# Whole rows of x in DRAM: four gathers per job, square turns on VectorE, and the stores of x issued by SyncE

## The chip, the core and the metric

The kernel runs on one core of a Trainium2 chip. The metric is the device time of one execution in microseconds; a profiled execution gives the span and the trace. A core has five engines that run their own instruction streams and wait for one another by semaphores: TensorE (PE; its weight loads are PEld), VectorE (DVE), ScalarE (ACT), GpSimd (POOL) and SyncE (SP). Data moves between DRAM and SBUF by DMA, on 16 DMA engines of the core.

## The reference, cut to what matters

Two blocks in a row. The first is a retention layer (4 batches, 8 heads, 768 positions, head width 64), the second a mixture of 8 experts over its 3072 output rows x of width 512, in which each token goes to one expert.

```python
for t in range(S):                                    # retention, per batch and head
    state = gamma[None, :, None, None] * state + np.einsum('bhd,bhe->bhde', k[:, :, t], v[:, :, t])
    y[:, :, t] = scale * np.einsum('bhd,bhde->bhe', q[:, :, t], state)
x = np.ascontiguousarray(y.transpose(0, 2, 1, 3)).reshape(B * S, H * D)

logits = x @ w_gate                                   # experts
expert_idx = np.argmax(logits, axis=1)
gate_w = probs[np.arange(N), expert_idx]              # softmax of logits
for e in range(E):                                    # x_sorted: rows of x sorted by expert
    h = np.maximum(x_sorted[lo:hi] @ w1[e], 0.0)      # 512 x 1024
    y_sorted[lo:hi] = h @ w2[e]                       # 1024 x 512
out = gate_w[:, None] * y_sorted[inv_perm]
```

## The kernel before

Attention runs in 24 steps (6 stretches of 128 positions times 4 batches). Each step leaves x transposed, features on partitions (`xTg`); VectorE turns its 32x32 blocks into `xg`, and after every four steps ScalarE's queue stores 1 MB of it to DRAM (`x_d`), as quarter rows of 128 numbers. `place` finds the expert and the place of each token. Then there is one job per expert: its rows are gathered from `x_d` by GpSimd, turned on VectorE into `xT`, and go through two layers on TensorE. One expert's gather is 16 indirect DMAs, each of 128 quarter rows. The first two experts' first 256 slots (`EARLY`) are gathered when five of the six groups of tokens are placed, and expert 0's early half runs its first layer while the last group is being placed. TensorE, ScalarE, GpSimd and VectorE keep the order of the text (`manual_schedule`); SyncE's order is the scheduler's.

```python
    L = 32
    Q = P // L
    x_d = dram.tile([N * Q, DT * L], F32, tag="x_d", name="x_d")
    # ... (cut)
    xs2 = [first.tile([P, W // L, DT * L], F32, tag=f"xs{i}", name=f"xs{i}") for i in range(2)]

    def gather(xs, idx, blocks, rows=N * Q):
        for b in blocks:
            nc.gpsimd.indirect_dma_start(
                out=xs[:, b, :], out_offset=None, in_=x_d[0:rows, :],
                in_offset=bass.IndirectOffsetOnAxis(ap=idx[:, b : b + 1], axis=0), bounds_check=rows - 1,
                oob_is_err=False)

    def tables(got, name):
        m = got.shape[2]
        hl = rt([P, 2, m], f"hl{name}", BF16)
        nc.vector.tensor_copy(hl, got[:, 0:2, :])
        ip = ps("tr", 3, "ip")[:, 0 : Q * 2 * m].rearrange("p (g i m) -> p g i m", g=Q, i=2)
        for g in range(Q):
            nc.tensor.matmul(ip[:, g, :, :].rearrange("p i m -> p (i m)"), lhsT=wrap[:, g, :],
                             rhs=hl[:, :, :].rearrange("p i m -> p (i m)"), start=True, stop=True)
        # ... (cut: six VectorE steps from ip to src: four row numbers for every slot)

    def turn(xs, xT, b0, b1):
        for dt in range(DT):
            nc.vector.transpose(xT[:, dt, :], xs[:, b0:b1, ts(dt, L)])

    hp_tags = [("sc", 2), ("sc", 2), ("lg", 1), ("tr", 3)]

    def layer1(n, xT, w1t, hT, f):
        hp = ps(*hp_tags[f % len(hp_tags)], "hp")[:, 0:n]
        for dt in range(DT):
            nc.tensor.matmul(hp, lhsT=w1t[:, 0, dt, ts(f, P)], rhs=xT[:, dt, 0:n], start=(dt == 0),
                             stop=(dt == DT - 1))
        nc.scalar.activation(out=hT[:, f, 0:n], in_=hp, func=AF.Relu)

    # ... (cut)
        def retain(n, then, between):
            c, b = steps[n]
            kt, vs, qT, kT = front.pop(n)
            sc = [ps("sc", 2, "sc").rearrange("p (a t) -> p a t", a=HP) for _ in range(2)]
            am = [att.tile([P, HP, P], F32, tag=f"am{j}", name=f"am{j}") for j in range(2)]
            for a in range(HP):
                for j in range(2):
                    r = ts(j, D)
                    nc.tensor.matmul(sc[j][:, a, :], lhsT=kT[r, a, :], rhs=qT[r, a, :], start=True, stop=True)
            for j in range(2):
                nc.vector.tensor_tensor(out=am[j], in0=sc[j], in1=middle(causal[:, :], HP), op=ALU.mult)
            then()
            # ... (cut: new state; y from the old state)
            between()
            for a in range(HP):
                for j in range(2):
                    nc.tensor.matmul(y[ts(j, D), a, :], lhsT=vs[:, 2 * a + j, :], rhs=am[j][:, a, :], start=(c == 0),
                                     stop=True, skip_group_check=True)
            nc.scalar.copy(out=xTg[n // B % 2][:, :, n % B, :], in_=y)

        def to_rows(n):
            g, b = n // B % 2, n % B
            nc.vector.transpose(xg[g][:, b, :, :].rearrange("p r (a l) -> p a r l", l=L),
                                xTg[g][:, :, b, :].rearrange("p a (r l) -> p a r l", l=L))

        def place(c):
            # ... (cut: logits of four steps, into PSUM tile parts)
            nc.scalar.copy(out=lgT, in_=parts)
            nc.scalar.dma_start(x_d[ts(c, B * P * Q), :].rearrange("(p r) d -> p r d", p=P),
                                xg[c % 2][:, :, :, :].rearrange("p b r d -> p (b r) d"))
            yield
            # ... (cut: expert, rank and place of each token, spread over the later steps; found, inv)
            if c == NC - 2:
                early.append(tables(inv[:, :, 0 : TC + HALF], "_e"))
                for e in range(2):
                    gather(xs2[e], early[0][0][:, e * TC * Q :],
                           range(HALF * Q), (c + 1) * B * P * Q)
    # ... (cut)
        actx.enter_context(tc.manual_schedule(engines={PE, ACT, POOL, DVE}))
        # ... (cut)
        for n in range(len(steps)):
            if n + AHEAD < len(steps):
                load(n + AHEAD)
            if n == len(steps) - AHEAD:
                wa = weights(first, 0)
            if n in (2, 3):
                nc.gpsimd.memset(xs2[n % 2], 0.0)
            if n + 2 < len(steps):
                scale(n + 2)
            # ... (cut: retain(n), with transpose(n + 1), to_rows(n - 1) and the next part of place in it)
        to_rows(len(steps) - 1)
        turn(xs2[0], xTa, 0, HALF * Q)
        cols = []
        for f in range(FT):
            layer1(EARLY, xTa, wa[0], hTa, f)
            if f in (0, 1, 2, 4):
                next(rest, None)
            if f == 3:
                arm, ne = count()
        src, dst, gates = tables(inv, "")
        cols = [(src[:, ts(e, TC * Q)], dst[:, ts(e, TC)], gates[:, ts(e, TC)]) for e in range(E)]
        for e in range(2):
            gather(xs2[e], cols[e][0], range(HALF * Q, TC * Q))
        turn(xs2[0], xTa, HALF * Q, TC * Q)
        layer2(EARLY, hTa, wa[1], oa, 0, early[0][2])
        which = regs(0)
        tc.switch_hint(which, arms_of(0), label="job0")
        layer2(EARLY, hTa, wa[1], oa, 1, early[0][2])
        scatter(oa, early[0][1], range(HALF))
    # ... (cut)
    def rows_of(e):
        xT = mp.tile([P, DT, W], F32, tag="xTs", name="xTs")
        if e > 1:
            gather(xs2[e % 2], cols[e][0], range(TC * Q))
        turn(xs2[e % 2], xT, 0, TC * Q)
        return xT
    # ... (cut)
    with tc.manual_schedule(engines={PE, ACT, POOL}):
        xT, xTn = xTa, rows_of(1)
        for e in range(E):
            last = e + 1 == E
            nxt = None if last else regs(e + 1)
            hT = mp.tile([P, FT, W], F32, tag="hT", name="hT", bufs=1)
            for a in tc.Switch(which, arms_of(e), hint=f"job{e}"):
                job(e, min(STEP * (LEAST + a), W), xT, hT, nxt)
                if last and a == arms_of(e) - 1:
                    further_jobs()
            if not last:
                scatter(o2[e % 2], cols[e][1], range(TC - HALF if e == 0 else TC))
                xT, which = xTn, nxt
            if e + 2 < E:
                xTn = rows_of(e + 2)
                sets.append(weights(first if e % 2 == 0 else keep2, e + 2))
```

## Time and profile before

The median of three runs is 566.6 us (565.68 to 570.61). The profiled execution has a span of 565.0 us.

| what | value |
|---|---|
| TensorE matmuls, busy | 501.0 us, 3008 records |
| GpSimd, busy | 215.1 us |
| VectorE, busy | 124.2 us |
| ScalarE, busy | 104.3 us |
| mean granted TensorE clock | 0.954 |
| gathers of the jobs (L174, src) | 112, 111.9 us of GpSimd |
| gathers of the early halves (L174, src_e) | 16, 16.2 us of GpSimd |
| stores of x (x_d<-xg, from ScalarE's queue) | 6 of 1024 KB, 5.2 us to landing |
| loads of k, v and q (from SyncE) | 24 of 256 KB, 24 of 256 KB, 12 of 512 KB |
| weights (from SyncE) | 16 of 2048 KB |
| DMA packets | 83224, 72.46 MB, of these 54712 under 512 B |

How to read the lines that follow. The page's slices cut the span into 40 equal parts of 14.1 us; a digit is the busy share in tenths, and PEclk is the TensorE clock that was granted. A line of a timeline has the start in us, the time that it covers in us, the engine, the line of the source, the operation, out<-in by the program's names, shapes, the number of instructions that it merges, and in brackets the idle time of the engine just before, with what ended it: an engine's work, a DMA, "issue" (nothing that the profile shows) or "remote" (a semaphore that no recorded instruction set). A line of a group has the count, then the busy time in us and the mean in ns of one, then the idle time before them and what ended most of it. A matmul of 32-bit numbers leaves two records.

### The profile page before, as it was taken

The page shows a single profiled execution, that of the slowest core. Times are in us where ns is not written, and L with a number is a line of the kernel's source. Part 1 is how long each engine was busy: PE and PEld are TensorE (multiplying, and loading weights), DVE is VectorE, ACT ScalarE, POOL GpSimd, SP SyncE. Part 2 cuts the span into 40 slices and gives each one's busy share as a digit, 9 for nine tenths or more (in the row PEclk, how much of TensorE's full clock was granted, in tenths as well). Part 3 has the DMA queues.
Part 4 walks back from the last instruction along what each step waited for, and adds up shares of the span by engine and source line. Part 5 has one row for each costly group of instructions (what it writes and reads, how often), then busy time and mean ns, then how long its engine had stood idle before and what let it go on. Part 6 is the DMA issues. An engine that isn't in the chain of part 4 may idle for free. (4 is left out here: it accounts for less than half of the span.)

```text
span 565.0 us, 7708 instructions
## 1 busy us (share of the span) xinstructions
PE 501.0 (89%) x3008; PEld 300.6 (53%) x3008; DVE 124.2 (22%) x356; ACT 104.3 (18%) x204; POOL 215.1 (38%) x232
## 2 busy tenths in 40 slices
PE   5998999996189959989969999999998899799992
PEld 4776888875156545544534454455454345345540
DVE  2468667675137110010010001000100100100000
ACT  2433242331011111120111012011011101011200
POOL 4744334414601734700760174057157007602010
PEclk9999999999579979989998999999999799999997
DMA  9999999911117118104610650192371047101010
GB/s 207 224 238 233 240 263 274 271 75 27 48 75 281 54 50 317 43 2 151 235 33 2 196 199 13 46 323 56 111 254 38 2 152 240 32 5 55 1 41 21
DMA packets 83224, 72.46 MB, mean 128 GB/s; under 512 B 54712, under 2 KB 67004, under 8 KB 82369
## 3 DMA queue, kind: packets, MB, share of 16 engines
q1 hardware_dynamic: 75472, 52.45, 34.4%
q0 software_dynamic: 6656, 12.61, 7.0%
q10 hardware_dynamic: 1008, 6.34, 3.0%
q8 instruction: 42, 0.69, 0.5%
q14 instruction: 46, 0.37, 0.2%
HBM read 60.88 MB, written 14.68 MB: 134 GB/s over the span
## 5 line engine op out<-in xcount | busy, mean ns | idle before, releaser
L247 PE MATMUL ye<-w2t,hT 128*128 128x512 f32 (+3 forms) x640 | 175.9, 481 | 16.4 <-issue 13.1
L235 PE MATMUL hp<-xTs,w1t 128*128 128x416 f32 (+3 forms) x448 | 154.4, 505 | 0.1
L247 PEld LDWEIGHTS ye<-w2t,hT 128*128 128x128 f32 (+3 forms) x640 | 79.6, 164 | 110.0 <-issue 104.6
L174 POOL DMA_INDIRECT xs<-x_d,src x112 | 111.9, 999 | 60.8 <-issue 33.8
L235 PEld LDWEIGHTS hp<-xTs,w1t 128*128 128x128 f32 x448 | 85.0, 190 | 69.6 <-issue 54.3
L257 POOL DMA_INDIRECT out_dram<-o,dst x30 | 29.8, 995 | 197.9 <-ACT o L253 169.7
L228 DVE STREAM_TRANSPOSE xTs<-xs 128x512 f32<-128x512 f32 x28 | 17.4, 680 | 284.8 <-DMA xs<-x_d,src 233.3
L237 ACT ACTIVATE hT<-hp 128x416 f32<-128x416 f32 (+4 forms) x64 | 29.1, 481 | 165.8 <-issue 75.9
L335 POOL TENSOR_TENSOR vs<-v,dec 128x512 f32<-128x512 f32 x23 | 25.3, 1102 | 55.0 <-DMA v<-in_v_dram 17.0
L235 PE MATMUL hp<-xTa,w1t 128*128 128x256 f32 (+1 forms) x128 | 27.5, 378 | 19.2 <-issue 11.2
L253 ACT ACTIVATE o<-ye,gate 128x512 f32<-128x512 f32 (+1 forms) x22 | 15.1, 687 | 125.8 <-PE ye L247 120.4
L361 DVE TENSOR_TENSOR am<-sc,causal 128x512 f32<-128x512 f32 x48 | 30.8, 681 | 32.0 <-PE sc L359 25.8
L388 PE MATMUL y<-am,vs 128*64 128x128 f32 x384 | 30.3, 291 | 5.8 <-issue 4.7
L235 PEld LDWEIGHTS hp<-xTa,w1t 128*128 128x128 f32 x128 | 22.7, 225 | 23.9 <-issue 14.0
L359 PE MATMUL sc<-qT,kT 64*128 64x128 f32 x384 | 28.8, 291 | 1.4 <-ACT qT L347 0.7
L388 PEld LDWEIGHTS y<-am,vs 128*64 128x64 f32 x384 | 23.0, 143 | 10.7 <-issue 6.1
L359 PEld LDWEIGHTS sc<-qT,kT 64*128 64x128 f32 x384 | 24.1, 193 | 4.9 <-issue 2.7
L390 ACT COPY xTg<-y 128x512 f32<-128x512 f32 x24 | 14.1, 586 | 66.0 <-PE y L388 44.6
L332 POOL TENSOR_TENSOR qs<-q,dec 128x512 f32<-128x512 f32 x22 | 22.5, 1043 | 7.7 <-DMA q<-in_q_dram 7.4
L174 POOL DMA_INDIRECT xs<-x_d,src_e x16 | 16.2, 1014 | 18.7 <-DVE at_e L210 14.2
L383 PE MATMUL y<-qT,state 64*64 64x128 f32 x320 | 21.8, 275 | 0.0
L321 PE MATMUL tr<-ident,k 128*128 128x128 f32 x96 | 16.2, 292 | 4.5 <-DMA k<-in_k_dram 4.5
(147 smaller groups left out, 273.9 us busy)
## 6 DMA issues: line engine op xcount, KB each, us to landing
w1t<-in_moe_w_dram SPq DMA_DIRECT2D x8, 2048.0 KB, 9.2
w2t<-in_moe_w_dram SPq DMA_DIRECT2D x8, 2048.0 KB, 14.3
k<-in_k_dram SPq DMA_DIRECT2D x24, 256.0 KB, 6.0
q<-in_q_dram SPq DMA_DIRECT2D x12, 512.0 KB, 5.7
v<-in_v_dram SPq DMA_DIRECT2D x24, 256.0 KB, 6.0
x_d<-xg ACTq DMA_DIRECT2D x6, 1024.0 KB, 5.2
xs<-x_d,src POOLq DMA_INDIRECT x112
out_dram<-o,dst POOLq DMA_INDIRECT x30
```

Of the source, the lines that this page charges most:

```text
L174: nc.gpsimd.indirect_dma_start(out=xs[:, b, :], out_offset=None, in_=x_d[0:rows, :], in_offset=bass.IndirectOffsetOnAxis(ap=idx[:, b : b + ...
L228: nc.vector.transpose(xT[:, dt, :], xs[:, b0:b1, ts(dt, L)])
L235: nc.tensor.matmul(hp, lhsT=w1t[:, 0, dt, ts(f, P)], rhs=xT[:, dt, 0:n], start=(dt == 0), stop=(dt == DT - 1))
L237: nc.scalar.activation(out=hT[:, f, 0:n], in_=hp, func=AF.Relu)
L247: nc.tensor.matmul(y[j * m : j * m + m, 0:c], lhsT=hT[:, f, t * P : t * P + m], rhs=w2t[:, 0, f, ts(j, c)], start=(f == 0), stop=(f == FT ...
L257: done = nc.gpsimd.indirect_dma_start(out=out[:, :], out_offset=bass.IndirectOffsetOnAxis(ap=idx[:, t : t + 1], axis=0), in_=o[:, t, :], i ...
L332: mul.tensor_tensor(out=qs[:, e, :, :], in0=got["q"][:, :, ts(e, D)], in1=inner(dec[:, ts(c + e, H)], D), op=ALU.mult)
L335: mul.tensor_tensor(out=vs, in0=got["v"], in1=inner(dec[:, ts(NC + c, H)], D), op=ALU.mult)
L359: nc.tensor.matmul(sc[j][:, a, :], lhsT=kT[r, a, :], rhs=qT[r, a, :], start=True, stop=True)
L361: nc.vector.tensor_tensor(out=am[j], in0=sc[j], in1=middle(causal[:, :], HP), op=ALU.mult)
L383: nc.tensor.matmul(y[r, a, :], lhsT=old[r, a, :], rhs=qT[r, a, :], start=(a == 0), stop=False, skip_group_check=True)
L388: nc.tensor.matmul(y[ts(j, D), a, :], lhsT=vs[:, 2 * a + j, :], rhs=am[j][:, a, :], start=(c == 0), stop=True, skip_group_check=True)
```

## The change

`x_d` now holds whole rows: 3072 rows of 512 numbers (2 KB) in place of 12288 quarter rows. A gather of 128 whole rows is one indirect DMA, so a job needs four of them instead of 16, and only one row number per slot instead of four: the four small matmuls with `wrap` and several VectorE steps of `tables` are not needed. What arrives has tokens on partitions, 512 features along the row, with the features in the order in which the stores left them. The 128-partition turns of before do not serve for this layout. A job's `xT` is made by 16 square turns on VectorE, one for each pair of a quadrant of 32 partitions to read and one to write. For expert 0's early half it is made in another way: two copies `xe` on VectorE that put the features in order, eight 128x128 turns on TensorE, and two copies out of PSUM. Expert 1's rows go to a buffer of their own (`xT1`), turned in two halves, so that its turn is no longer part of `rows_of`.

To get whole rows into DRAM, a store of four steps becomes four DMAs, one per quadrant of `xg`, each from 32 partitions in pieces of 128 numbers. They are issued by SyncE and no longer by ScalarE, at a fixed place among the loads, since SyncE's order is now that of the text too. The first expert's weights are loaded two steps later in the text, behind all loads of k, q and v. The diff, cut:

```diff
@@ -89,8 +89,7 @@
     Q = P // L
 
-
-    x_d = dram.tile([N * Q, DT * L], F32, tag="x_d", name="x_d")
+    x_d = dram.tile([N, Q * DT * L], F32, tag="x_d", name="x_d")
 
 
@@ -133,20 +132,12 @@
     row_i, row_r, row_l, tile_4 = (rt([P, 1], "row_i", I32), rt([P, 1], "row_r", I32), rt([P, 1], "row_l", I32),
                                    rt([P, NT], "tile_4"))
-    quarter = rt([P, 1], "quarter")
... (cut)
-
-    wrap = rt([P, Q, P], "wrap", BF16)
-    nc.gpsimd.memset(wrap, 1.0)
-    nc.gpsimd.affine_select(out=wrap[:, :, :].rearrange("p g (a l) -> p g a l", l=L),
-                            in_=wrap[:, :, :].rearrange("p g (a l) -> p g a l", l=L), compare_op=ALU.is_equal,
-                            fill=0.0, base=0, pattern=[[-L, Q], [0, Q], [-1, L]], channel_multiplier=1)
     ohs = rt([P, NT, E], "ohs", BF16)
     ranks = rt([P, NT], "ranks", I32)
@@ -166,54 +157,37 @@
 
     first = ctx.enter_context(tc.tile_pool(name="first", bufs=1))
-    xs2 = [first.tile([P, W // L, DT * L], F32, tag=f"xs{i}", name=f"xs{i}") for i in range(2)]
-
-    def gather(xs, idx, blocks, rows=N * Q):
-
-        for b in blocks:
+    xs2 = [first.tile([P, TC, Q * DT * L], F32, tag=f"xs{i}", name=f"xs{i}") for i in range(2)]
+
+    def gather(xs, idx, tiles, rows=N):
+        for t in tiles:
             nc.gpsimd.indirect_dma_start(
-                out=xs[:, b, :], out_offset=None, in_=x_d[0:rows, :],
-                in_offset=bass.IndirectOffsetOnAxis(ap=idx[:, b : b + 1], axis=0), bounds_check=rows - 1,
+                out=xs[:, t, :], out_offset=None, in_=x_d[0:rows, :],
+                in_offset=bass.IndirectOffsetOnAxis(ap=idx[:, t : t + 1], axis=0), bounds_check=rows - 1,
                 oob_is_err=False)
 
 
         m = got.shape[2]
-        hl = rt([P, 2, m], f"hl{name}", BF16)
-        nc.vector.tensor_copy(hl, got[:, 0:2, :])
-        ip = ps("tr", 3, "ip")[:, 0 : Q * 2 * m].rearrange("p (g i m) -> p g i m", g=Q, i=2)
-        for g in range(Q):
-            nc.tensor.matmul(ip[:, g, :, :].rearrange("p i m -> p (i m)"), lhsT=wrap[:, g, :],
-                             rhs=hl[:, :, :].rearrange("p i m -> p (i m)"), start=True, stop=True)
... (cut: removed, the six VectorE steps from ip to src)
-        return (src,) + targets(got, name)
-
-    def targets(got, name):
+        tok, far = rt([P, m], f"tok{name}"), rt([P, m], f"far{name}")
+        src = rt([P, m], f"src{name}", U32)
+        nc.vector.tensor_scalar(out=far, in0=got[:, 0, :], scalar1=1.0, scalar2=float(FAR), op0=ALU.is_lt, op1=ALU.mult)
+        nc.vector.tensor_tensor(out=far, in0=got[:, 1, :], in1=far, op=ALU.add)
+        nc.vector.scalar_tensor_tensor(out=tok, in0=got[:, 0, :], scalar=float(L), in1=far, op0=ALU.mult, op1=ALU.add)
+        nc.vector.tensor_scalar(out=src, in0=tok, scalar1=-float(L), scalar2=None, op0=ALU.add)
+        return (src,) + targets(got, far, name)
+
+    def targets(got, far, name):
... (cut: far is now made in tables)
@@ -222,10 +196,14 @@
         return dst, gate
 
-    def turn(xs, xT, b0, b1):
-
-        for dt in range(DT):
-            nc.vector.transpose(xT[:, dt, :], xs[:, b0:b1, ts(dt, L)])
+    def turn(xs, xT, tiles):
+
+        n = len(tiles)
+        for r in range(Q):
+            for g in range(Q):
+                nc.vector.transpose(
+                    xT[ts(g, L), :, 0 : n * P].rearrange("p a (t r i) -> p r t a i", r=Q, i=L)[:, r, :, :, :],
+                    xs[ts(r, L), tiles[0] : tiles[0] + n, ts(g, P)].rearrange("p t (a i) -> p t a i", i=L))
 
     hp_tags = [("sc", 2), ("sc", 2), ("lg", 1), ("tr", 3)]
@@ -408,8 +386,9 @@
             lgT = att.tile([P, B * P], F32, tag="lgT", name="lgT", bufs=1)
             nc.scalar.copy(out=lgT, in_=parts)
-            nc.scalar.dma_start(x_d[ts(c, B * P * Q), :].rearrange("(p r) d -> p r d", p=P),
-                                xg[c % 2][:, :, :, :].rearrange("p b r d -> p (b r) d"))
+            for g in range(Q):
+                nc.sync.dma_start(x_d[ts(c, B * P), ts(g, P)].rearrange("(t l) r -> l t r", l=L),
+                                  xg[c % 2][ts(g, L), :, :, :].rearrange("p b q r -> p (b q) r"))
             yield
             lg = ps("lg", 1, "lg")[:, 0 : B * E].rearrange("p (b e) -> p b e", e=E)
@@ -490,8 +469,7 @@
                 early.append(tables(inv[:, :, 0 : TC + HALF], "_e"))
                 for e in range(2):
-                    gather(xs2[e], early[0][0][:, e * TC * Q :],
-                           range(HALF * Q), (c + 1) * B * P * Q)
+                    gather(xs2[e], early[0][0][:, e * TC :], range(HALF), (c + 1) * B * P)
 
                 tot = ps("tr", 3, "tot")[:, 0:2]
@@ -504,19 +482,20 @@
         for n in range(AHEAD):
             load(n)
-        actx.enter_context(tc.manual_schedule(engines={PE, ACT, POOL, DVE}))
+        actx.enter_context(tc.manual_schedule(engines={PE, ACT, POOL, DVE, SP}))
         for n in range(2):
             scale(n)
         nc.sync.dma_start(wg[:, :, 0:E], w_gate.rearrange("(dt p) e -> p dt e", p=P))
         xTa = first.tile([P, DT, EARLY], F32, tag="xTa", name="xTa")
+        xT1 = first.tile([P, DT, W], F32, tag="xT1", name="xT1")
         hTa = keep.tile([P, FT, EARLY], F32, tag="hTa", name="hTa")
         oa = keep.tile([P, EARLY // P, DM], F32, tag="oa", name="oa")
             if n + AHEAD < len(steps):
                 load(n + AHEAD)
-            if n == len(steps) - AHEAD:
+            if n == len(steps) - 3:
                 wa = weights(first, 0)
             if n in (2, 3):
@@ -538,10 +517,19 @@
                 rest = place(n // B)
         to_rows(len(steps) - 1)
-        turn(xs2[0], xTa, 0, HALF * Q)
+
+        xe = keep.tile([P, HALF, DM], F32, tag="xe", name="xe")
+        for t in range(HALF):
+            nc.vector.tensor_copy(xe[:, t, :].rearrange("p (a q l) -> p q a l", q=Q, l=L),
+                                  xs2[0][:, t, :].rearrange("p (q a l) -> p q a l", q=Q, l=L))
 
 
         cols = []
+        for t in range(HALF):
+            tr = ps("tr", 3, "tre").rearrange("p (a t) -> p a t", a=DT)
+            for dt in range(DT):
+                nc.tensor.transpose(tr[:, dt, :], xe[:, t, ts(dt, P)], ident)
+            nc.vector.tensor_copy(xTa[:, :, ts(t, P)], tr)
         for f in range(FT):
             layer1(EARLY, xTa, wa[0], hTa, f)
@@ -549,10 +537,12 @@
                 arm, ne = count()
         src, dst, gates = tables(inv, "")
-        cols = [(src[:, ts(e, TC * Q)], dst[:, ts(e, TC)], gates[:, ts(e, TC)]) for e in range(E)]
+        cols = [(src[:, ts(e, TC)], dst[:, ts(e, TC)], gates[:, ts(e, TC)]) for e in range(E)]
         for e in range(2):
-            gather(xs2[e], cols[e][0], range(HALF * Q, TC * Q))
-        turn(xs2[0], xTa, HALF * Q, TC * Q)
+            gather(xs2[e], cols[e][0], range(HALF, TC))
+        turn(xs2[1], xT1, range(HALF))
+        turn(xs2[0], xTa, range(HALF, TC))
+        turn(xs2[1], xT1[:, :, EARLY:], range(HALF, TC))
 
         cols[0] = (None, dst[:, HALF:TC], gates[:, HALF:TC])
@@ -585,9 +575,8 @@
 
         xT = mp.tile([P, DT, W], F32, tag="xTs", name="xTs")
-        if e > 1:
-            gather(xs2[e % 2], cols[e][0], range(TC * Q))
-        turn(xs2[e % 2], xT, 0, TC * Q)
+        gather(xs2[e % 2], cols[e][0], range(TC))
+        turn(xs2[e % 2], xT, range(TC))
         return xT
 
@@ -660,7 +649,7 @@
 
     with tc.manual_schedule(engines={PE, ACT, POOL}):
-        xT, xTn = xTa, rows_of(1)
+        xT, xTn = xTa, xT1
         for e in range(E):
             last = e + 1 == E
```

## The prediction

> **What bounds the kernel now.** I read the page's busy shares and slices first, then the timeline of all engines where the slices dip, then TensorE's timeline through the jobs, then the groups.
>
> ```profile
> PE 501.0 (89%) x3008; PEld 300.6 (53%) x3008; DVE 124.2 (22%) x356; ACT 104.3 (18%) x204; POOL 215.1 (38%) x232
> ...
> PE   5998999996189959989969999999998899799992
> ...
> PEclk9999999999579979989998999999999799999997
> ```
>
> TensorE is the bound: 501 of 565 us, nine tenths in most slices. So a change gains only in the dips: slices 10 and 11 (141 to 155 us), 14 (198 to 212), and the weak ones in the jobs. The granted clock falls to a half in the same places. The chain of waits holds only the last microsecond and does not help.
>
> ```profile
> 138.43 0.58 ACT L390 COPY xTg<-y 128x512 f32<-128x512 f32 x1 [4.89 <-PE sc L359]
> ...
> 142.73 1.40 DVE L361 TENSOR_TENSOR am<-sc,causal 128x512 f32<-128x512 f32 x2 [6.22 <-remote]
> ...
> 143.57 2.58 PE L388 MATMUL y<-am,vs 128*64 128x128 f32 x16 [4.73 <-issue]
> ...
> 152.42 1.00 POOL L174 DMA_INDIRECT xs<-x_d,src_e  x1 [0.30 <-issue]
> ...
> 155.61 0.58 ACT L390 COPY xTg<-y 128x512 f32<-128x512 f32 x1 [16.59 <-remote]
> ...
> 157.37 2.90 PE L235 MATMUL hp<-xTa,w1t 128*128 128x256 f32 x6 [11.22 <-issue]
> ```
>
> This is the end of attention, in order of time. VectorE waits for the scores sc, whose matmuls stand in the trace at 136.66 to 137.8, and starts at 142.73. ScalarE waits for y, whose matmuls end at 146.15, and starts at 155.61. Both wait 5 to 9.5 us longer than any work that I see, and "remote" says that no recorded instruction released them. What does run there is GpSimd: 16 gathers at a pitch of 1.30 us, 132.6 to 153.4. ScalarE wakes 2.2 us after the last one ended. TensorE idles 4.73 + 11.22 = 16 us. The same picture stands at 197 to 203: TensorE idles 6.03 us for ScalarE, which idles 8.75 us on "remote", while 16 gathers and 2 scatters run from 180.4 to 203.5.
>
> ```profile
> 289.34 1.06 PE L247 MATMUL ye<-w2t,hT 128*32 128x128 f32 x27
> 291.37 0.27 PE L247 MATMUL ye<-w2t,hT 128*32 128x128 f32 x1 [0.97 <-issue]
> ...
> 294.21 0.27 PE L247 MATMUL ye<-w2t,hT 128*32 128x128 f32 x1 [1.73 <-issue]
> ...
> 296.31 24.44 PE L247 MATMUL ye<-w2t,hT 128*32 128x128 f32 x80 [0.98 <-issue]
> ...
> 531.80 22.75 PE L247 MATMUL ye<-w2t,hT 128*32 128x128 f32 x112
> ```
>
> These are second layers of jobs of one size (416 rows, 112 matmul records). The last job has no gathers beside it and takes 22.75 us; job 2 takes 290 to 321, 31.2 us, stammers until 296.31, and then runs some us at half clock. The gathers of job 2 end at 293.86. I take gathers on GpSimd as what holds back TensorE's signals: the stalls end about 2 us after the last gather in every case (243.5 after 241.3, 296.3 after 293.9, 441.6 after 439.4). Why is not in the profile.
>
> ```profile
> L174 POOL DMA_INDIRECT xs<-x_d,src x112 | 111.9, 999 | 60.8 <-issue 33.8
> ...
> L257 POOL DMA_INDIRECT out_dram<-o,dst x30 | 29.8, 995 | 197.9 <-ACT o L253 169.7
> L228 DVE STREAM_TRANSPOSE xTs<-xs 128x512 f32<-128x512 f32 x28 | 17.4, 680 | 284.8 <-DMA xs<-x_d,src 233.3
> ```
>
> A gather moves 128 pieces of 512 B and costs GpSimd 999 ns; a scatter moves 128 rows of 2 KB and costs 995. The cost is by instruction, not by bytes.
>
> [...] mean granted clock 0.58 over 138 to 158, 0.81 over 192 to 210. [...]
>
> **The change, part by part.**
>
> *Gathers.* 16 per job become 4 of whole 2 KB rows. At 1.30 us pitch, 20.8 us of GpSimd become 5.2. Both are hidden as GpSimd time; what counts is how long they lie beside TensorE.
>
> *End of attention.* The index table loses four matmuls and some VectorE steps, so the first gather goes at about 131.5 instead of 132.6, and the last ends at 136.7. The rows land by 138.5 (2 us after, as above). Then, at the trace's durations: sc done 137.8, mask 1.3 to 139.2, y 1.1 to 140.4, xTg 0.6 to 141.1, xg 0.7 to 141.8. New on the path: two copies xe, about 0.5 us each (a guess from 0.70 for 512 elements of turn, and the clear of 2048 at 1.76), eight TensorE turns of 128x128 (1.04 us for eight in attention's row), two evictions at about 0.69 (the mask from PSUM took 0.68). The first hp starts at about 145, against 157.37. I add 1 us for a remaining late signal and 2 us for attention itself (below): 148, a gain of 9.5.
>
> *First layer of the early half.* 157.37 to 177.78 = 20.4 us, of which 4.3 us ran at half clock, worth 2.1. Without the index matmuls (0.8) and with 1 us of cold clock left: 18.3 - 0.8 + 0.3 = about 18. Second layer starts near 166 and ends 14 us later, near 180 (191.75 before).
>
> *Turns.* One 128-partition turn of 256 elements takes 0.40 us alone, 0.33 in a row; a 32-partition turn has as many elements per lane. So a half of 16 square turns is 16 x 0.42 = 6.7 us, and a whole job 16 x 0.70 = 11.2 us, against 1.4 and 2.5. The three halves stand in line after the tables (done near 168): 175, 181.5, 188. The second is what job 0 needs: 181.5 against 180, a new wait of 1.5 us. The job turns are hidden: gathers land about 14 us into a job, 11 us of turns end at 25, and jobs take 40 to 54 us.
>
> *Job 0.* Starts 181.5 (192.33 before). Its stall of 6.03 + 0.78, and about 2.6 us lost to the half clock from 202.6 to 209.4, go, but for 1 us. First layer 7.4, second 7.0: job 1 starts near 197.5, against 216.47. Gain so far 19.
>
> *Jobs 1 to 6.* Second layers against what the same shapes take undisturbed (22.75 for 416 rows; 3 x 6.87 = 20.6 for three tiles; 24.0 for 448): 28.0 - 22.75 = 5.2, 31.2 - 22.75 = 8.5, 25.8 - 24.0 = 1.8, 20.6 - 20.6 = 0, 31.8 - 22.75 = 9.0, 24.0 - 20.6 = 3.4. Sum 27.9. The four gathers now end 11 us into the job, inside the first layer, which has PSUM buffers for four columns ahead (4 x 2.8 = 11.2 us). I count 23 of the 28.
>
> *Stores of x.* 6 of 1 MB, pieces of 8 KB from all partitions, become 24 of 256 KB from 32 partitions, pieces of 512 B. In the trace 8 KB pieces took 351 ns (768 of them: 16.8 us of all 16 DMA engines) and 512 B loads 32 ns; 12288 x 32 / 16 = 24.4 us. So +7.6 us of DMA in a front that is at a DMA share of about 1.0 to 110 us. But the 4 MB of the first expert's weights, 13 us, move behind all loads, and from 51 us on SyncE waits for free buffers, not for engines. What suffers is 33 to 50 us, where GpSimd waits for v and q: +2 us.
>
> Sum: 19 + 23 = 42 off 566.6: **525 us**.
>
> **Rivals.** (1) The late signals are not the gathers' doing, or come with any four of them: then the stalls stay or move into the first layer. For it: scatters (2 KB rows) lie at the start of each job, and the first hT there comes 7.9 us after the job's start against 5.3 in job 7. Against: the stalls' ends follow the last gather. It leaves about 13 us of the gain (earlier rows alone): 550. (2) SyncE or the DMA engines become attention's bound, since stores wait in the line of the loads [...]. For it: DMA share of 1.0 now. Against: stores land only after data that the loads no longer need, and weights leave that stretch. It costs perhaps 10 to 15 us: 538. (3) VectorE becomes the bound between the halves: if a square turn costs 0.7 rather than 0.42, job 0 waits 9 us more and the clock drops: 536. (4) All stalls go: 516.
>
> **Range and chances.** The middle is 525; (4) and a faster tail give 511 as low end, (2) or (3) or half of (1) give 548 as high end. Slower by 2% would need attention to lose 50 us. Faster by over 2% (below 555) 0.91, within 2% 0.06, slower 0.03.
>
> **What would show it.** Right: 32 gathers in the group, of about 1.0 us; no "remote" waits over 3 us on ScalarE; first hp near 148; second layers of 416 rows near 23 us in every job; clock at 1.0 through the jobs; a row of turns of 32 partitions near 0.4 and 0.7 us. Wrong: stalls of TensorE that stay in the second layers though no gather runs; GpSimd's waits for v and q growing before 60 us; TensorE waiting for xTa.

## The result, and the profile after

The changed kernel takes 519.86 us (median of 4; 518.46 to 521.32) against 566.71 us: ratio 0.916, 95% interval 0.912 to 0.9205. The prediction was 525, in 511 to 548. The stalls that it read off the profile are gone. But the experiments will show that the 46.8 us depend on something outside the program: beside some of them the kernel before, unchanged, took 517 us.

Busy time, TensorE's slices and the granted clock, from the page of the changed kernel:

```profile
PE 484.8 (94%) x3008; PEld 293.2 (57%) x3008; DVE 194.4 (38%) x457; ACT 104.5 (20%) x204; POOL 117.9 (23%) x134
...
PE   4998999999789699999999999999999999999991
...
PEclk9999999999999989999999999999999999999996
```

TensorE works as many instructions as before (3008) in 484.8 us instead of 501.0, with a mean granted clock of 0.989 instead of 0.954; the span fell from 565.0 to 516.7. Slices 10, 11 and 13, counted from 0 (129 to 155 and 168 to 181 us), stay weak. In order of time, all engines at the end of attention:

```profile
136.57 1.00 POOL L164 DMA_INDIRECT xs<-x_d,src_e  x1 [0.30 <-issue]
...
138.26 1.29 DVE L339 TENSOR_TENSOR am<-sc,causal 128x512 f32<-128x512 f32 x2 [2.21 <-PE sc L337]
139.10 1.59 PE L366 MATMUL y<-am,vs 128*64 128x128 f32 x16 [0.72 <-DVE am L339]
...
140.73 0.59 ACT L368 COPY xTg<-y 128x512 f32<-128x512 f32 x1 [2.69 <-PE y L366]
...
142.43 1.09 PE L531 MATMUL tre<-ident,xe 128*128 128x128 f32 x8 [1.73 <-DVE xe L523]
```

These answer to the lines of the end of attention before. The last of four gathers ends at 137.57, not 153.42. The mask waits for sc until 138.26, not 142.73. ScalarE copies y at 140.73, not 155.61, and its releaser is a TensorE instruction, not "remote". Next, TensorE's own timeline, with the early half, job 0 and a second layer of 416 rows:

```profile
144.47 1.99 PE L213 MATMUL hp<-xTa,w1t 128*128 128x256 f32 x8 [0.94 <-DVE xTa L532]
...
161.85 13.90 PE L225 MATMUL ye<-w2t,hTa 128*128 128x512 f32 x32
...
179.98 9.01 PE L213 MATMUL hp<-xTa,w1t 128*128 128x128 f32 x64 [4.24 <-DVE xTa L204]
...
263.17 22.75 PE L225 MATMUL ye<-w2t,hT 128*32 128x128 f32 x112
```

The first hp is 12.9 us earlier than before. Job 2's second layer is one unbroken row of 112 matmuls in 22.75 us; before, it stammered for 31.2. A new wait stands ahead of job 0: 4.24 us for a turn of xTa. From the groups:

```profile
L204 DVE STREAM_TRANSPOSE xTs<-xs 32x512 f32<-32x512 f32 x96 | 67.4, 702 | 191.4 <-DMA xs<-x_d,src 190.2
```

The square turns of jobs 2 to 7 take 702 ns each, 11.2 us a job, all of it hidden.

One more view, worked out from the trace's semaphore events: how long after the modelled end of a TensorE instruction its semaphore next rose on record. In the kernel before, some 60 instructions are over 0.5 us late, more than half of them over 3 us, the worst 12.42 us. In the changed kernel there are 9, three over 3 us, the worst 6.03. I call these late signals. The count must not be taken as it stands, because the traces lack events: the kernel before has 340 of TensorE's on record, and a later trace of the same program 358. An event that is missing looks late. ScalarE in job 2 of the kernel before, where the 12.42 us stand:

```profile
274.80 1.33 ACT L237 ACTIVATE hT<-hp 128x416 f32<-128x416 f32 x3 [7.01 <-issue]
278.27 0.52 ACT L237 ACTIVATE hT<-hp 128x416 f32<-128x416 f32 x1 [2.14 <-issue]
...
294.92 0.52 ACT L237 ACTIVATE hT<-hp 128x416 f32<-128x416 f32 x1 [6.51 <-issue]
```

The signal that seems 12.42 us late is that of a column that ended at 275.44, but ScalarE reads this column at 275.61, as the third of the first row. The last line is truly late: its column ended at 289.41, 5.5 us before. So the start of the reader is the surer measure, beside the same read in a trace of the same program in which no signal is late (both kernels have such a trace below). By it, 14 of ScalarE's 72 reads of first-layer columns are over 1 us late in the kernel before, up to 10.3 us; in the changed kernel none is, the worst 0.9. Nor is every stall a wait for a signal: 10.0 us of TensorE's idle time in the kernel before, in 16 pieces, stand ahead of second-layer matmuls that wait for no semaphore, as do the 1.73 us at 294.21 in the prediction's lines.

### The profile page after: what moved, and what is told of

Read it like the earlier page. It is cut to its first block, busy times and chain, and to the rows that moved or that the text cites. A ratio compares the mean times of both kernels' runs of the same rounds, so it can differ in the third digit from the quotient of the medians.

```text
span 516.7 us, 7619 instructions
## 1 busy us (share of the span) xinstructions
PE 484.8 (94%) x3008; PEld 293.2 (57%) x3008; DVE 194.4 (38%) x457; ACT 104.5 (20%) x204; POOL 117.9 (23%) x134
## 5 line engine op out<-in xcount | busy, mean ns | idle before, releaser
L225 PE MATMUL ye<-w2t,hT 128*128 128x512 f32 (+3 forms) x640 | 164.0, 455 | 0.0
L204 DVE STREAM_TRANSPOSE xTs<-xs 32x512 f32<-32x512 f32 x96 | 67.4, 702 | 191.4 <-DMA xs<-x_d,src 190.2
L213 PE MATMUL hp<-xTs,w1t 128*128 128x416 f32 (+3 forms) x384 | 131.9, 504 | 0.0
L225 PEld LDWEIGHTS ye<-w2t,hT 128*128 128x128 f32 (+3 forms) x640 | 74.9, 155 | 86.5 <-issue 85.0
L213 PEld LDWEIGHTS hp<-xTs,w1t 128*128 128x128 f32 x384 | 72.9, 190 | 59.1 <-issue 44.0
L164 POOL DMA_INDIRECT xs<-x_d,src x28 | 28.4, 1014 | 34.9 <-DVE at L186 26.7
L366 PE MATMUL y<-am,vs 128*64 128x128 f32 x384 | 28.6, 281 | 1.6 <-DVE am L339 1.4
L213 PE MATMUL hp<-xTa,w1t 128*128 128x256 f32 (+1 forms) x128 | 24.1, 350 | 5.8 <-DVE xTa L204 4.2
L213 PEld LDWEIGHTS hp<-xTa,w1t 128*128 128x128 f32 x128 | 20.5, 208 | 9.2 <-issue 5.9
L213 PE MATMUL hp<-xT,w1t 128*128 128x416 f32 x64 | 22.5, 512 | 0.0
```

The source lines that it names most:

```text
L164: nc.gpsimd.indirect_dma_start(out=xs[:, t, :], out_offset=None, in_=x_d[0:rows, :], in_offset=bass.IndirectOffsetOnAxis(ap=idx[:, t : t + ...
L204: nc.vector.transpose(xT[ts(g, L), :, 0 : n * P].rearrange("p a (t r i) -> p r t a i", r=Q, i=L)[:, r, :, :, :], xs[ts(r, L), tiles[0] : t ...
L225: nc.tensor.matmul(y[j * m : j * m + m, 0:c], lhsT=hT[:, f, t * P : t * P + m], rhs=w2t[:, 0, f, ts(j, c)], start=(f == 0), stop=(f == FT ...
```

## Experiments

My theory was the prediction's: a run of 16 gathers on GpSimd holds back TensorE's signals. The first four kernels were meant to separate the number of gathers from the rest of the change, and from the mere busyness of GpSimd.

**Sixteen gathers in the new layout.**

```diff
+        quarters = x_d[:, :].rearrange("n (g r) -> (n g) r", g=Q)
         for t in tiles:
-            nc.gpsimd.indirect_dma_start(out=xs[:, t, :], in_=x_d[0:rows, :], ...)
+            for g in range(Q):                                          # index 4 * src + g
+                nc.gpsimd.indirect_dma_start(out=xs[:, t, ts(g, P)], in_=quarters[0 : rows * Q, :], ...)
```

> The changed kernel with each gather of 128 whole rows split into four gathers of 128 quarter rows (512 B), so 16 per job again, same bytes, same layout, same square turns, stores and TensorE turns; three more small VectorE steps per table. Theory (the run of 16 gather instructions on GpSimd, 20.8 us, holds back TensorE's signals): second layers of 416 rows at 28 to 32 us again in jobs 1 to 6 instead of 22.75, some 25 us lost there, and the end of attention waits for the last gather again, some 13 us: about 558 us. Rival (the stalls went for another reason: the whole rows, the square turns, the stores' queue): only the early rows come later, 13 us, second layers stay at 22.75: about 533 us.

**A quarter of the gathers in the kernel before.**

```diff
-        for b in blocks:
+        for b in list(blocks)[::Q]:     # three quarters of the rows of x are left out
```

> The kernel before with only every fourth gather (4 of 16 per job, 128 pieces of 512 B each); the other three quarters of the rows are left out, all else is as it was. Theory: the stalls go without any other part of the change: second layers of 416 rows 22.75 us in every job, no wait over 3 us on ScalarE or VectorE that no instruction released at the end of attention, first hp near 143 to 146: 515 to 525 us. Rival (whole rows, turns or stores are what removed the stalls): the early half starts earlier by up to 13 us, the jobs keep their 28 us: about 550 us.

**Clears on GpSimd in place of gathers**, on the changed kernel:

```diff
         # after the loop of gathers
+        for i in range(5 * len(tiles)):
+            nc.gpsimd.memset(ballast, 0.0)                              # 128 x 800
```

> The changed kernel with five clears of 128x800 on GpSimd after each gather's tile group (20 per job, about 0.75 us each, some 15 us), so that GpSimd is busy as long as with 16 gathers, with no DMA in it. Theory (making gathers, not a busy GpSimd, holds back TensorE's signals): second layers stay at 22.75 us, 520 to 522 us. Rival (any long stretch of work on GpSimd does it): 540 to 560 us.

**Plain transfers by GpSimd in place of gathers**, on the changed kernel:

```diff
         # after the loop of gathers
+        for i in range(3 * len(tiles)):
+            nc.gpsimd.dma_start(plain[:, i, :], x_d[0:P, 0:L])          # 128 pieces of 128 B
```

> The changed kernel with three plain GpSimd transfers (128 pieces of 128 B from fixed rows of x, no index) after each gather, 12 per job beside the four gathers. Theory in its wider form (any transfer that GpSimd issues does it, by its number of pieces): about 1 us each, second layers of 28 us and more again, 540 to 560 us. Narrow form (only gathers by index do it): second layers stay at 22.75 us, 520 to 523 us.

Measured: sixteen gathers 527.52 us, a quarter of the gathers 510.33, clears 521.37, plain transfers 518.29 (12 runs from 514.4 to 520.9). But the kernel before took **516.63 us** beside them, in the same session (kernels run one after the other on one chip), not 566.7, so the ratios to it are 1.021 (1.0168 to 1.0248), 0.990 (0.9861 to 0.9936), 1.010 (1.0072 to 1.0128) and 1.003 (0.9998 to 1.0055). In none of the four traces is a signal over 0.5 us late, and in all the second layers of 416 rows take 22.75 us. By its own numbers my theory fell, since 16 gathers brought no stall; they only bring the rows later (first hp at 149.15, against 144.47 in the changed kernel). Clears and plain transfers could tell nothing, as nothing was late. So I ran the two kernels of the case again, unchanged, and with them an improvement: the turn for job 0 first.

**The kernel before, and the changed kernel, again** (no edit).

> The kernel before, unchanged, once more with a profile, because beside the first experiments it took 516.6 us and not 566.7. New theory: the late signals of TensorE are not in the program alone; on the chip of those experiments even a run of 16 gathers does not bring them. Then the profile shows second layers of 416 rows at 22.75 us in every job, no wait over 3 us without a recorded releaser, a first hp still near 155 because the rows still come after the sixteenth gather, and 515 to 518 us. Rival (my first theory): 16 gathers always bring the stalls, and the time is near 566 us with second layers of 28 to 32 us.

> The changed kernel, unchanged, beside the kernel before on one chip. New theory: where the kernel before has no stalls, the change gives earlier rows and pays square turns: 518 to 521 us against 516.6, that is equal or up to 1 per cent slower. Rival: it stays 8 per cent faster, 520 against 566 us.

**The turn of xTa first.**

```diff
-        turn(xs2[1], xT1, range(HALF))
         turn(xs2[0], xTa, range(HALF, TC))
+        turn(xs2[1], xT1, range(HALF))
```

> The changed kernel with the turn of the second half of job 0 (xTa) put ahead of the turn of the first half of job 1 (xT1), so that job 0 no longer waits for a turn that only job 1 needs. Theory: TensorE's wait of 4.24 us for xTa goes, since its rows land near 168 and 7.2 us of turns end near 175.7, as the second layer does; job 1's two turns end near 190, before job 1 starts: 4 to 6 us less than the changed kernel, 514 to 516 us. Rival (the gathers land too late or job 1 then waits): within 2 us of the changed kernel.

Measured: the kernel before took 516.79 us (24 runs), and its profiled run 517.83; the changed kernel took 519.67, ratio 1.005 (1.0034 to 1.0067): **slower by half a per cent**. The timeline of the kernel before in this run:

```profile
139.83 0.59 ACT L390 COPY xTg<-y 128x512 f32<-128x512 f32 x1 [2.97 <-PE y L388]
...
144.72 3.75 PE L235 MATMUL hp<-xTa,w1t 128*128 128x256 f32 x8 [4.93 <-issue]
...
151.93 1.00 POOL L174 DMA_INDIRECT xs<-x_d,src_e  x1 [0.30 <-issue]
...
263.11 22.75 PE L247 MATMUL ye<-w2t,hT 128*32 128x128 f32 x112
```

It is the same program with the same 16 gathers, of 1.00 us at the same pitch of 1.30. But ScalarE copies y at 139.83 (155.61 in the first trace), TensorE starts the first hp at 144.72, while gathers still run and not near 155 as I expected, and job 2's second layer takes 22.75 us. There is no late signal. TensorE idles 30.2 us, against 64.0 in the first trace, and is busy for 485.9, against 501.0: together the 48.9 us between the spans. So 16 gathers are not enough: something outside the program decides whether they hurt.

The two traces differ in one more thing. The first trace has 2560 packets of 4 bytes for GpSimd's 160 transfers, 16 each, but only 682 events of their landing; here 2556 are on record. In four traces the profile has no time to landing for the gathers: the first ones of both kernels, and below the second one of sixteen gathers and the second one of the mixed loads. All four were taken where the kernel before took 566 us; but where it took as long or longer, the improved kernel (4.5 us) and the one with its stores on ScalarE (4.2 us) have it. What loses the events, and whether the recording itself has a part in the stalls, was not tested.

Turning xTa first gave 516.74 us, 2.9 less than the changed kernel beside it; I had expected 4 to 6. Job 0 in the changed kernel beside it, and with the new order:

```profile
180.32 10.27 PE L213 MATMUL hp<-xTa,w1t 128*128 128x128 f32 x64 [4.24 <-DVE xTa L204]
```

```profile
179.90 7.38 PE L213 MATMUL hp<-xTa,w1t 128*128 128x128 f32 x64 [2.68 <-DVE xTa L204]
```

The wait fell from 4.24 to 2.68 only, because VectorE now waited 5.54 us for the rows of the last gathers, which landed at 172.6 and not near 168. More came from the clock: the same 64 matmuls take 7.38 us, not 10.27. The granted clock at job 0 is at half for 3.413 us in the changed kernel's first profile, for 6.827 here, after the same wait of 4.24 us, and not at all in the new order, which has 3.413 us at the first hp. (At the end of all three spans it is at half again, in the first for 8.1 us.) A half-clock stretch follows a wait of 2.12 us below, and none the wait of 2.68 us here. So a few microseconds come and go for the same wait, and I read differences of that size from the waits, not from totals.

**An improved kernel, and sixteen gathers once more.** VectorE's two clears of o (1.76 us each) stood ahead of the last table step, and so of the gathers that job 0 waits for.

```diff
 # on top of the turn of xTa first
-        nc.vector.memset(t, 0.0)           # the two o tiles
+        nc.gpsimd.memset(t, 0.0)
 # and to_rows(len(steps) - 1) moved from before the two copies xe to after them
```

> The changed kernel with the turn of xTa first, the two clears of o moved from VectorE to GpSimd (they stand ahead of the last table step), and the copies xe ahead of the last turn of xg. Theory: on VectorE 3.5 us of clears go from the path to the last gathers, so these go some 3 to 4 us earlier, their turn ends before TensorE's second layer does, and the 2.7 us that TensorE still waited for xTa go; tre starts some 0.7 us earlier: 512 to 514 us, faster than the changed kernel by 1 per cent or more, and than the kernel before by 0.5 per cent or more where that one takes 517. Rival (GpSimd's clears now hold the gathers, or clears beside the turns slow VectorE): 516 to 518 us.

> The changed kernel with 16 gathers of quarter rows per job once more, on another occasion. What it does is read beside the kernel before. If that one takes 517 us here too, this one takes 524 to 529 us with second layers of 22.75 us. If that one takes 566 us here, the theory that 16 gathers bring late signals there says 550 us or more, with second layers of 28 to 32 us; the rival, that whole rows or square turns removed them, says 524 to 535 us.

Here the kernel before took **566.37 us** (11 runs) again. The improved kernel took 515.47, ratio 0.909 (0.9046 to 0.913), and sixteen gathers in the new layout took **572.05** (one run), as the theory says and the rival does not. The timeline of sixteen gathers, at the end of attention and in job 2:

```profile
153.29 0.99 POOL L166 DMA_INDIRECT xs<-x_d,src_e  x1 [0.30 <-issue]
156.46 0.58 ACT L372 COPY xTg<-y 128x512 f32<-128x512 f32 x1 [17.28 <-remote]
...
289.58 0.99 PE L229 MATMUL ye<-w2t,hT 128*32 128x128 f32 x24
...
295.16 0.40 PE L229 MATMUL ye<-w2t,hT 128*32 128x128 f32 x1 [1.85 <-issue]
296.54 24.40 PE L229 MATMUL ye<-w2t,hT 128*32 128x128 f32 x84 [0.98 <-issue]
```

The marks of the kernel before's first trace are back: "remote" for 17.28 us, ending 2.2 us after the last gather's end, and the stammer in job 2. So in such a session the number of gather instructions brings the late signals (15 reads of first-layer columns are over 1 us late, up to 8.6), whatever the layout, the turns or the stores; the same kernel took 527.52 in the first session, with none.

In the improved kernel, TensorE's timeline:

```profile
143.57 1.99 PE L213 MATMUL hp<-xTa,w1t 128*128 128x256 f32 x8 [1.49 <-DVE xTa L532]
...
176.98 9.01 PE L213 MATMUL hp<-xTa,w1t 128*128 128x128 f32 x64 [2.12 <-DVE xTa L204]
```

The first hp comes 0.9 us earlier than in the changed kernel (144.47), job 0 3.0 us earlier. Not all of the wait went, since VectorE still waits 5.89 us for the rows, and the 2.12 us that are left cost a stretch of 3.413 us at half clock. Expected were 512 to 514. It is 0.8% below the changed kernel of either session, which was not run beside it. In a session without late signals it was not run; turning xTa first equals the kernel before there (0.999, 0.9975 to 1.0005).

**What in the gathers does it.** One kernel gives each job's second layer another GpSimd load, on the changed kernel:

```diff
         for t in tiles:
-            nc.gpsimd.indirect_dma_start(out=xs[:, t, :], ..., ap=idx[:, t : t + 1])
+            for r in range(Q if kind == "short" else 1):    # beside jobs 1 and 3; three quarters of the rows left out
+                a, b = (r * L, r * L + L) if kind == "short" else (0, P)
+                nc.gpsimd.indirect_dma_start(out=xs[a:b, t, :], ..., ap=idx[0 : b - a, t : t + 1])
+        for i in range(25 if kind == "plain" else 20):
+            if kind == "clear":                             # beside jobs 4 and 5
+                nc.gpsimd.memset(ballast, 0.0)              # 128 x 800
+            if kind == "plain":                             # beside jobs 2 and 6
+                nc.gpsimd.dma_start(ballast[:, ts(i, L)], x_d[0:P, 0:L])
```

> The changed kernel with another GpSimd load beside each job, to tell apart what in a long run of gathers makes TensorE's signals late, where they are late at all (a kernel before near 566 us beside it; near 517 us it can tell nothing, and every second layer is at its shape's undisturbed time). Beside jobs 1 and 3: the four gathers cut into 16 of 32 rows of 2 KB (same bytes; the rows of the first 32 stand for all, so part of the rows is left out). Beside jobs 2 and 6: four gathers and 25 plain transfers issued by GpSimd, 128 pieces of 128 B each, about 13.5 us. Beside jobs 4 and 5: four gathers and 20 clears of 128x800, about 15 us. With 16 gathers of quarter rows where signals were late, second layers took 26.4, 31.2, 27.1, 20.8, 32.8 and 27.0 us in jobs 1 to 6 against 22.75, 22.75, 24.47, 20.76, 22.75 and 20.76 undisturbed. Theory ([...]): jobs 2 and 6 stall by 4 us or more each, job 5 does not, jobs 1 and 3 follow the time that the short gathers take (near none if a gather of 32 rows takes a third of one of 128). Rival A (any long work on GpSimd): job 5 stalls by 5 us or more. Rival B (only gathers by index, by their number): jobs 1 and 3 stall by 2 us or more, jobs 2, 5 and 6 not.

> The same kernel of mixed GpSimd loads on another occasion, because on the first one the kernel before took 517 us and no signal was late. If the kernel before takes near 566 us beside it, the theory and rivals say what they said: [...] by rival A (any long work on GpSimd) job 5 stalls by 5 us or more; by rival B (gathers by index, by their number) jobs 1 and 3 stall by 2 us or more and jobs 2, 5 and 6 not. If the kernel before takes 517 us again, this one takes 515 to 519 us and the question stays open.

The first time the kernel before took 517.02 us and this one 516.23, with every second layer undisturbed and no late signal: no answer. The second time the kernel before stood at 566.37 and this one took 526.39. GpSimd's timeline, then TensorE's second layers:

```profile
219.72 0.91 POOL L168 DMA_INDIRECT xs<-x_d,src  x1 [0.30 <-issue]
...
265.48 10.54 POOL L176 DMA_DIRECT2D ballast<-x_d  x20 [0.64 <-DMA xs<-x_d,src]
...
398.00 16.42 POOL L174 MEMSET ballast<- 128x800 f32 x20
```

```profile
220.92 0.62 PE L234 MATMUL ye<-w2t,hT 128*32 128x128 f32 x10
...
225.37 25.02 PE L234 MATMUL ye<-w2t,hT 128*32 128x128 f32 x100 [0.34 <-issue]
...
272.67 22.75 PE L234 MATMUL ye<-w2t,hT 128*32 128x128 f32 x112
...
319.41 1.94 PE L234 MATMUL ye<-w2t,hT 128*64 128x256 f32 x14
...
324.49 22.77 PE L234 MATMUL ye<-w2t,hT 128*64 128x256 f32 x64 [0.34 <-issue]
...
409.07 22.75 PE L234 MATMUL ye<-w2t,hT 128*32 128x128 f32 x112
```

From the start of its second layer to the start of the next job, job 1 took 29.3 us (220.92 to 250.23; undisturbed 22.6) and job 3 took 27.7 (319.41 to 347.10; undisturbed 24.3): the two with 16 gathers. Jobs 2, 4, 5 and 6 took their undisturbed times. Beside the kernel's first trace, ScalarE reads first-layer columns up to 10.0 us later in job 1 and 9.6 in job 3; in the other jobs no read is over 0.5 us later. So rival B holds, in this one run: 16 gathers by index in a row do it, and four do not (numbers between were not tried). Long clears do not do it, nor do 25 plain transfers of 128 pieces each. These took 14.4 us (261.59 to 276.02), though, against 19.1 us of short gathers, so a longer row of plain transfers remains untried. My theory in its wide form (a long run of transfers by GpSimd, by index or not) fell, since jobs 2 and 6 did not stall.

**The stores' queue**, on the improved kernel:

```diff
-                nc.sync.dma_start(x_d[ts(c, B * P), ts(g, P)] ...
+                nc.scalar.dma_start(x_d[ts(c, B * P), ts(g, P)] ...
```

> The improved kernel of the run before (turn of xTa first, clears of o on GpSimd, xe ahead of the last xg) with the 24 stores of x issued by ScalarE again instead of SyncE. Where SyncE issues them, found of the fifth group of attention stands at 130.2 to 131.5 us in eight traces; in the kernel before, with its stores on ScalarE, at 128.9 to 129.6 in three. Theory (stores in the line of the loads hold the loads back): found comes 1 to 1.5 us earlier, 129.3 to 129.8, and the whole takes 513.5 to 515 us. Rival (the 512 B pieces cost their DMA time whoever issues them): found stays at 130.2 to 131.5 and the whole at 515 to 516.5 us.

The kernel before took 578.62 us beside it, this one 515.75 (ratio 0.890, 0.8866 to 0.894): within the rival's 515 to 516.5, and no gain over SyncE. But found stands outside both expectations, from the timeline of all engines:

```profile
99.95 6.84 ACTq L390 DMA_DIRECT2D x_d<-xg  x4
...
107.44 0.58 ACT L320 COPY kT<-tr 128x512 f32<-128x512 f32 x1
108.07 0.18 PE L417 MATMUL rk<-ohs,before 128*128 128x32 bf16 x1 [2.31 <-ACT kT L320]
```

ScalarE needs 6.84 us to issue four of these stores (3.4 to 6.8 for the whole groups during attention), its copies xTg and kT wait for that, and TensorE waits 2.31 us for kT. Found comes at 132.96, later than in any other trace. SyncE takes 3.40 us for four in the improved kernel, but has no copies to make. The late start is partly given back: TensorE waits only 1.17 us for xTa ahead of job 0, and its first layer there runs at full clock, 7.38 us instead of 9.01.

## Why the prediction was right, and where it was not

**The cause of the dips.** Right in the conditions it was made for, incomplete in general. In sessions where the kernel before takes 566 to 579 us, 16 gathers break the second layers, in the old and in the new layout, and four leave them smooth in the new one (in the old layout, four were run only in the other kind of session). In sessions where it takes 517 us, 16 gathers bring no stall. That the pair was timed where signals are late was luck: in the other kind of session the change is 0.5% slower, and nothing in the prediction could tell. It said that why was not in the profile. It is still open: the program, the gathers' durations and their pitch are the same in both kinds of session. Held-back signals are also not all of it, since 10.0 us of TensorE's idle time wait for none. The split in measured terms, across sessions: the stalls with their half clock cost the kernel before 566.7 - 516.8 = 49.9 us and the changed kernel nothing that shows (519.86 and 519.67); all the rest of the change costs 519.67 - 516.79 = 2.9 us; 49.9 - 2.9 = 47.0 is the whole gain of 46.8.

**"The cost is by instruction, not by bytes"** held, and the number of rows is hardly in it either: a gather of 32 rows took 0.90 to 0.96 us against 1.00 for 128.

**End of attention: first hp at 148, gain 9.5.** It came at 144.47, gain 12.9. The sum before the two allowances said about 145; the 1 us for a remaining late signal and 2 us for attention were hardly drawn on (found of the fifth group came at 130.19 against 129.56, and the copies xe took 0.36 us each, not 0.5).

**The step that was wrong** is the reading of that gain as earlier rows, which rival (1) put at "about 13 us of the gain (earlier rows alone)". Expert 0's early half needs only the first eight of the 16 gathers. Without late signals the kernel before has its first hp at 144.72, and the changed one at 144.81 in the same session. The changed kernel without late signals, and in a second trace the kernel before with a quarter of the gathers:

```profile
144.81 1.99 PE L213 MATMUL hp<-xTa,w1t 128*128 128x256 f32 x8 [0.94 <-DVE xTa L532]
```

```profile
141.70 1.97 PE L235 MATMUL hp<-xTa,w1t 128*128 128x256 f32 x8 [1.79 <-issue]
```

Earlier rows gain nothing in sum, because xe, the TensorE turns and their evictions take up what they give: the second kernel needs none of these and starts at 141.70. What stalled the first hp was the signal of y. So rival (1)'s 550 was a false number; had the late signals stayed, the change would have shown no gain, as sixteen gathers suggest (572 against 566).

**First and second layer of the early half**: 17.4 us against about 18, and 13.90 against 14.

**Turns.** 16 x 0.42 = 6.7 us for a half was 7.2 (165.48 to 172.65), 16 x 0.70 for a job was right. Counting full durations, 0.42 and not the 0.33 of the turns in a row before, was right: a half turn lasts 0.436 us on average and they follow one another at 0.448, so nothing overlaps. Why was not shown.

**Job 0's wait of 1.5 us was 4.24**, and its first layer took 9.01 us, not 7.4, with 3.413 us at half clock, which the prediction did not foresee for so short a wait. The turns ended at 179.84, close to the 181.5 foreseen; but the second layer ended at 175.75, not 180, as the first hp had come 3.5 us earlier. I carried the allowances into one chain and not into the wait between the two. Rival (3) was right about the engine and wrong about the cause: the queue of halves, not a slow turn.

**Jobs 1 to 7: 23 us.** They gave 28.3 (195.70 to 505.45 is 309.75 us, against 338.1), the full 27.9 and a little more. I had kept back 5 us for gathers that still lie beside the first layer. There no column is read over 0.9 us later than in the kernel's other trace (the 6.03 us on record, of a column that started at 294.40, are a missing event), so the allowance was not needed. With that, rival (4), all stalls go, came nearest: 516 against 519.9.

**Stores: +2 us on attention.** In the measured pair it was 0.6. Over ten traces with the stores on SyncE, found stands at 130.2 to 131.5, and at 128.9 to 129.6 in three with the old stores: some 1.8 us, so the size was right. Which part is the line of the loads and which the 512 B pieces stays open. ScalarE was worse, for a third reason.

**Rival (2)**, attention bound by SyncE or DMA, did not come. Two slips change nothing: 12288 x 32 / 16 is 24.6 us, not 24.4, and 141 to 155 us is slice 10 alone, counted from 0.

## What to carry to other kernels

Fewer, larger gathers by index are worth more than their GpSimd time: here they cost by instruction (1.00 us for 128 pieces of 512 B and for 128 of 2 KB), and a row of 16, but not of four, held TensorE up and made its signals late in some sessions (31.2 us for job 2's second layer, against 22.75). An engine that waits on "remote" though its producer has long finished was the sign of it here (16.59 us on ScalarE in the kernel before); take how late it is from the start of the waiting engine, since events can be missing from a trace (682 on record against 2556 for one program). A stall that the program does not explain may also not be the program's: time the old kernel beside every experiment, since the same change was worth 8% in one session and cost 0.5% in another. And when a step moves one of two chains that meet, predict the wait between them anew, and not each end by itself.

## What was unexpected in the hardware

- One program, the kernel before, took 516.6, 516.8 and 517.0 us in three sessions and 566.4, 566.7 and 578.6 beside others. Where both were traced, one trace has late signals and the other none. What sets them is open: chips recorded under the same number showed both.
- In sessions with late signals, columns of TensorE beside a row of 16 indexed gathers were read up to 10.3 us late in the kernel before and 10.0 us beside the mixed loads; there, beside 25 plain GpSimd transfers (0.54 us each) and 20 clears (16.42 us in all), none was over 0.5 us late.
- Traces of one program differ in the semaphore events on record: for the landings of GpSimd's 160 transfers (2560 packets of 4 bytes) the kernel before has 682 in its first trace and 2556 in its trace without late signals.
- In the kernel before, 16 idle pieces of TensorE, 10.0 us, stand before matmuls that wait for no semaphore; in its trace without late signals there are none.
- An indexed gather of 32 rows of 2 KB costs GpSimd 0.91 us, one of 128 rows 1.00.
- Four stores of 256 KB from 32 partitions took ScalarE 3.4 to 6.8 us to issue during attention; one 1 MB store from all partitions took it 0.33.
